# A planned two-branch kernel: other pairs in seven-product form, another order of the input splits, two rows normed on GpSimd, longer planned transposes

## The chip, the core and the metric

The kernel runs on one core of one Trainium2 chip. Its time is the device time of one execution in microseconds (us). The profile adds one recorded execution, in which every instruction of every engine has a start and an end. The engines are TensorE (PE in the profile), VectorE (DVE), ScalarE (ACT), GpSimd (POOL) and SyncE (SP), which only issues DMAs.

## The reference

```python
xn = _layernorm(x, axis=-1)                       # x = A_q, 2048 rows of 1024
return x + _A_ref(xn, ...) + _B_ref(xn, B_w1, B_w2)

# _A_ref: k_shift is a 4-tap causal convolution of k by channel
kv = k_shift * v
y = irfft(rfft(pad(kv)) * rfft(pad(ssm_k)))[:S]   # a long causal convolution by channel
y = y + kv * ssm_D
return xn * y

# _B_ref
h = silu(xn @ w1)                                 # w1 is 1024 x 3584
return h @ w2                                     # w2 is 3584 x 1024
```

All inputs and outputs are float32. There are 2048 rows, 1024 channels and 3584 hidden columns.

## The kernel before

**Two branches, one TensorE.** The feed-forward branch (B) is two large products; the convolution branch (A) runs as transforms, whose first stages are products with constant matrices. All products are made from float16 halves: a value is scaled and split into a high part (ScalarE, L355) and a low part (VectorE, L347, the function `split`), and each product takes three matmuls, high by high, high by low and low by high. L930 to L932 are these three of the first feed-forward product, L1062 to L1064 of the second, L1529 to L1531 of the convolution's forward transform (constants `cfw`), L1721 to L1723 of its inverse (`civ`).

**Seven products for eight.** The normed input is cut into 2 by 2 blocks, A11 to A22, by halves of its rows and of its columns, and so is each 256-column pair of w1, B11 to B22. Sums of blocks (S1 to S4 of the input, T1 to T4 of the weights) let a unit make its block products from seven products P1 to P7 (`PRODUCTS`) in place of eight. The hidden columns are 14 such pairs. In the first half of the rows, pairs 0 and 1 are done as plain products ahead of all others, because their operands are there first: first with A11 and A12 (rows 0 to 3), then with A21 and A22 (rows 4 to 7). Units 2 to 13 follow, and then units 0 to 13 for the second half of the rows (rows 8 to 15).

**Pairs.** The second product, h by w2, is itself made in seven-product form for four of the 14 pairs, those in `PAIRS`. For them the activations need further sums and splits on VectorE and ScalarE, written by `quad`; the others take `blocks`. The hidden columns of the other ten pairs (`PLAIN`) go through the plain second product, and those of `PAIRS` come last of all.

**The start.** `ln_rows` takes statistics of rows (`bn_stats`, L497 and L499), a square root on ScalarE, and applies the norm with one VectorE `tensor_scalar` a row (L516). `transposes` turns the rows with TensorE into PSUM (L535; a ring of three buffers). `first_rows` splits A11 and A12; `lower_sums` makes A21, A22 and S1, `upper_sums` makes S2, S3 and S4, and `give` hands each to a `split`. `scales_w1` finds the scale of a weight pair with `norm` (a matmul at L451 and a chain of small VectorE operations), and `factors_w1` makes and splits its factors. The eight places `x0` to `x7` in SBUF are shared: places 0 and 1 first hold the raw weights of pairs 0 and 1, and later S1 and S4 (`XPLACE`).

**The convolution.** For each of eight groups of 128 channels, `signal_parts` splits the signal into the one buffer `cm`; a transposing DMA (`X`, L337) moves it into `hl`, where the matmuls of the forward transform read it; `cm` can be refilled only when that DMA has read it. Sums on VectorE over `spec` and `tmp`, a product of the spectra and an inverse follow, and `gated` writes the result with an accumulating DMA issued by GpSimd (`G`, L341; tile `yt`, or a free `wo`). The results of the second product reach the output by such DMAs too.

**A planner sets every queue.** The kernel is written as many streams (Python generators) that yield operations, `Op(engine, busy, late, emit, reads, writes, margin)`. `Order.run` takes again and again the operation that could start first by its own model of time, less a `bias` of its stream, and emits it. So the order of the instructions on each engine follows from the costs and biases that the streams declare. Where the model sees TensorE idle, it puts filler matmuls in (L327):

```python
if op.fill is not None and t > 45.0:
    for _ in range(int(((t - self.free[op.eng]) * 0.7 - 0.3) / 0.22)):
        op.fill()
```

For a DMA the model takes the later of `busy + late` and a common pipe of all DMAs:

```python
self.pipe = max(self.pipe, t + 3.0) + op.nbytes / 330e3
done = end = max(end, self.pipe + 0.2)
```

The hardware runs each engine's queue in that order, and an instruction waits for what it needs.

Of the kernel before, what the change touches and what calls it, by code (L numbers as in the profile page):

```python
# [13 lines left out]
F16 = mybir.dt.float16  # L14
I32 = mybir.dt.int32
AF = mybir.ActivationFunctionType
# [23 lines left out]
            "P5": ("S1", "T1"), "P3": ("S4", "B22"), "P4": ("A22", "T4")}  # L40
XPLACE = dict(A11=2, A12=3, A22=5, S1=0, S2=6, S3=7, S4=1)

PAIRS = (8, 9, 12, 13)
NQ = len(PAIRS)
PLAIN = [j for j in range(NF) if j // 2 not in PAIRS]
NC = len(PLAIN) // 4
# [59 lines left out]
class Order:  # L106
# [27 lines left out]
    def add(self, gen, bias, floor=0.0):  # L134
        s = Stream(gen, bias, floor)
        self.streams.append(s)
        self.advance(s)
# [154 lines left out]
def h3_ffn_kernel(ctx, tc, x, kp, vs, fs, shift, dskip, w1, w2, cfwd, cinv, out):  # L292
# [23 lines left out]
    def V(f, o, ins, us=None, m=0.15):  # L316
        return Op("DVE", us or 1.03 * (size(o) / 960 + 0.075), 0.16, f, ins, [o], m)
# [16 lines left out]
    def X(o, i, m=0.3):  # L334

        n = size(o) * o.shape[0] * mybir.dt.size(o.dtype)
        return Op("SP", 0.6, 0.1, lambda: nc.sync.dma_start(o, i, transpose=True), [i], [o], m, n)  # L337

    def G(o, i, m=0.3):
        n = size(i) * i.shape[0] * mybir.dt.size(i.dtype)  # L340
# [135 lines left out]
    def load_row(t):  # L476
# [5 lines left out]
            yield L(xts[t][0][:, q], xr[t // T2, t % T2][:, q])  # L482
        flag["xt", t].set()

    def ln_rows():
        for t0, n, bias in ((0, 2, 0.26), (2, 2, 0.17), (4, 4, 0.15), (8, 8, 0.03)):
            yield bias
            q = slice(t0, t0 + n)
            mv = lnp.tile([P, 2, 8], F32, name="mv", bufs=2)
            m = mv[:, :, 0:n]  # L490
            order_in = (8, 9, 12, 13, 10, 11, 14, 15) if n == 8 else range(t0, t0 + n)
            for t in order_in:
                yield flag["xt", t]
                xt = xts[t][0]
                st = lnp.tile([P, 2, 6], F32, name="st", bufs=2)
                for a in range(2):
                    yield V(lambda: nc.vector.bn_stats(st[:, a, :], xt[:, a * W:(a + 1) * W]), st[:, a, :],  # L497
                            [xt[:, a * W:(a + 1) * W]], us=0.65)
                yield V(lambda: nc.vector.bn_aggr(stat[:, t, :], st), stat[:, t, :], [st], us=0.2)  # L499

            def chain(m=m, q=q):
                v = stat[:, q, 1]
                nc.vector.reciprocal(m[:, 0, :], m[:, 0, :])
                nc.vector.tensor_mul(m[:, 1, :], m[:, 0, :], m[:, 0, :])
                nc.vector.scalar_tensor_tensor(m[:, 1, :], v, 1e-5, m[:, 1, :], op0=ADD, op1=MUL)
                nc.vector.tensor_scalar(m[:, 1, :], m[:, 1, :], -0.5, 1.5, op0=MUL, op1=ADD)
                nc.vector.tensor_mul(rstd[:, q], m[:, 0, :], m[:, 1, :])
                if n == 8:
                    nc.vector.scalar_tensor_tensor(nmr, stat[:, :, 0], -1.0, rstd, op0=MUL, op1=MUL)
            yield a_act(m[:, 0, :], stat[:, q, 1], AF.Sqrt, bias=eps)  # L510
            p = V(chain, rstd[:, q], [stat[:, q, :], m[:, 0, :]], us=0.8)
            p.writes += [m[:, 0, :], m[:, 1, :]] + ([nmr] if n == 8 else [])
            yield p
            for t in order_in:
                xt = xts[t][0]
                yield V(lambda: nc.vector.tensor_scalar(xt, xt, stat[:, t, 0:1], rstd[:, t:t + 1], op0=SUB, op1=MUL),  # L516
                        xt, [xt, stat[:, t, :], rstd[:, t:t + 1]], us=0.78)
                flag["xn", t].set()

    pts = []  # L520
# [56 lines left out]
    def give(to, name, src, tok):  # L577

        put = to(name)
        if put is None:  # L580
            tok.set()
        else:
            add(put(src, tok), to.bias)

    def lower_sums(to, ring):

# [36 lines left out]
    def x_rows():  # L623
        yield from first_rows()
        second["A21"], second["tok"] = places[4].tile([P, 4, KH, 2, P], F16)
        for name in ("A22", "S2", "S3", "S1", "S4"):
            r = places[XPLACE[name]]
            yield r.ready
            xo[0][name], xtok[0][name] = r.tile([P, 4, KH, 2, P], F16)

        class Kept:
            bias = 0.14

            def __init__(self, i):
                self.i = i

            def __call__(self, name):
                if name in ("A11", "A12"):
                    return None
                o = (second["A21"] if name == "A21" else xo[0][name])[:, self.i]  # L640
                return lambda src, tok: split(o[:, :, 0], o[:, :, 1], src, XS, (tok, flag["x", 0, name]))

        yield 0.14
        half = []
        for i in range(4):
            half.append((yield from lower_sums(Kept(i), s1_r)))
        Kept.bias = 0.11
        yield 0.11
        for i in range(4):
            yield from upper_sums(Kept(i), xst_r, *half[i], t=i)  # L650

        class Spilled(Kept):
            bias = 0.02

            def __call__(self, name):
                return None if name == "A21" else lambda src, tok: spill(xsp[name][:, self.i], src, tok)

        def spill(o, src, tok):
            yield lambda: s1_r.ready() or xst_r.ready()
            r = s1_r if s1_r.ready() else xst_r  # L660
            st, stok = r.tile([P, KH, 2, P], F16)
            yield from split(st[:, :, 0], st[:, :, 1], src, XS, (tok,))
            yield L(o, st)
            stok.set()
            flag["spilled"].set()

        yield 0.02
        for i in range(4):
            part = yield from lower_sums(Spilled(i), sums_r)
            yield from upper_sums(Spilled(i), sums_r, *part)  # L670
        flag["x done"].set()
# [34 lines left out]
    def scales_w1():  # L706
        for n, (_, i) in enumerate(pairs):
            yield (0.25, 0.16, 0.1, 0.05)[min(n, 3)]
            m = 4 if n == 0 else 2
            if n >= NP:  # L710
                for a in range(m):
                    yield flag["raw", n, a]
                flag["scaled", n].set()
                continue
            yield sq_r.ready
            ss, tok = sq_r.tile([P, 4])
            for a in range(m):
                yield flag["raw", n, a]
                r = raws[n][2][a]
                yield a_act(junk[:, 0:r.shape[1]], r, AF.Square, total=ss[:, a:a + 1])  # L720

            def then(e, i=i):
                sc = wsc[:, i]
                nc.vector.tensor_scalar(sc[:, 3:5], powers[:, 3:5], e, None, op0=MUL)
                nc.vector.reciprocal(e, e)
                nc.vector.tensor_scalar(sc[:, 0:3], powers[:, 0:3], e, None, op0=MUL)
            yield from norm(ctxs["nm"], ss[:, 0:m], (m,), then, ([wsc[:, i]], [flag["scaled", n], tok]))

    spills = []

# [1067 lines left out]

    warm = lnp.tile([P, 1], F32, name="warm")
    nc.scalar.activation(warm, ones[:, 0:1], AF.Sqrt)  # L1800
    add(begin(), 0.05)
    add(warm_up(), 0.0)
    add(x_rows(), 0.03)
# [53 lines left out]
```

## Time and profile before

| | |
|---|---|
| runs | 1257.01, 1260.42, 1257.72 us |
| median of the three | 1257.72 us |
| the profiled execution's own time | 1257.19 us |
| its span, first to last instruction | 1255.4 us |
| mean granted TensorE clock | 0.996 |
| TensorE busy | 1233.6 us (98%) |
| VectorE busy | 1147.3 us (91%) |
| ScalarE busy | 731.0 us (58%) |
| GpSimd busy | 132.6 us (11%) |

A busy time is the union of an engine's instructions. A row of the time line gives start, duration, engine, line, operation, what it writes and reads, and in square brackets how long the engine stood idle before it and what released it. A row of waits gives who waited for whom, the total in us, how often, and the longest. One kernel matmul of float32 operands shows as two records.

### The profile page before, as it was taken

The page shows a single profiled execution, that of the slowest core. Times are in us where ns is not written, and L with a number is a line of the kernel's source. Part 1 is how long each engine was busy: PE and PEld are TensorE (multiplying, and loading weights), DVE is VectorE, ACT ScalarE, POOL GpSimd, SP SyncE. Part 2 cuts the span into 40 slices and gives each one's busy share as a digit, 9 for nine tenths or more (in the row PEclk, how much of TensorE's full clock was granted, in tenths as well). Part 3 has the DMA queues.
Part 4 walks back from the last instruction along what each step waited for, and adds up shares of the span by engine and source line. Part 5 has one row for each costly group of instructions (what it writes and reads, how often), then busy time and mean ns, then how long its engine had stood idle before and what let it go on. Part 6 is the DMA issues. An engine that isn't in the chain of part 4 may idle for free.

```text
span 1255.4 us, 17118 instructions
## 1 busy us (share of the span) xinstructions
PE 1233.6 (98%) x6058; PEld 599.7 (48%) x6058; DVE 1147.3 (91%) x1517; ACT 731.0 (58%) x1165; POOL 132.6 (11%) x141
## 2 busy tenths in 40 slices
PE   7999999999999999999999999999999999899998
PEld 6544554444444544445444544544454454345444
DVE  7999997999899979999999899989989979898994
ACT  6868887878767776748752632463173264426222
POOL 0000000000000020002010300210030030113114
PEclk9999999999999999999999999999999999999999
DMA  9358889889999998879998887699597578978777
GB/s 334 94 185 293 288 297 315 285 278 325 337 335 281 264 286 262 267 224 239 352 316 209 168 270 180 147 265 263 116 220 172 129 171 245 227 157 140 163 143 92
DMA packets 254293, 292.93 MB, mean 233 GB/s; under 512 B 48768, under 2 KB 167808, under 8 KB 252032
## 3 DMA queue, kind: packets, MB, share of 16 engines
q1 hardware_dynamic: 227472, 266.93, 67.9%
q0 software_dynamic: 26736, 24.92, 15.5%
q8 instruction: 47, 0.77, 0.2%
q14 instruction: 38, 0.31, 0.1%
HBM read 193.22 MB, written 98.57 MB: 232 GB/s over the span
## 4 chain that ended last, share of the span: by engine, by line
PE 72%; DVE 9%; DMA 5%; issue 2%; ACT 1%; POOL 0%; SPq 0%; DVEq 0%; ACTq 0%; POOLq 0%
PE ff L1062 11%; PE ff L1063 11%; PE ff L1064 11%; PE ff L930 11%; PE ff L931 11%; PE ff L932 11%; DVE spec L344 3%; DMA hl<-cm 2%; PE ps L1529 2%; PE ps L1531 2%; PE ps L1530 2%; DVE x L347 1%; DMA out<-yt 1%; DVE acc L347 1%; PE ps L1723 1%
## 5 line engine op out<-in xcount | busy, mean ns | idle before, releaser
L1062 PE MATMUL ff<-x,wo 128*128 128x512 f16 x868 | 328.8, 379 | 3.8 <-ACT hf L355 3.2
L1063 PE MATMUL ff<-x,wo 128*128 128x512 f16 x868 | 328.8, 379 | 0.0
L1064 PE MATMUL ff<-x,wo 128*128 128x512 f16 x868 | 328.6, 379 | 0.0
L931 PE MATMUL ff<-x,wo 128*128 128x512 f16 (+1 forms) x808 | 303.4, 375 | 2.7 <-DVE x L347 2.7
L932 PE MATMUL ff<-x,wo 128*128 128x512 f16 (+1 forms) x808 | 303.5, 376 | 1.9 <-DVE wo L347 1.9
L930 PE MATMUL ff<-x,wo 128*128 128x512 f16 (+1 forms) x808 | 303.5, 376 | 1.5 <-ACT wo L355 1.5
L344 DVE TENSOR_TENSOR spec<-spec 128x1024 f32<-128x1024 f32 (+2 forms) x272 | 263.6, 1000 | 2.7
L1063 PEld LDWEIGHTS <-wo 128*128 128x128 f16 x868 | 85.0, 98 | 103.8 <-issue 4.8
L1064 PEld LDWEIGHTS <-wo 128*128 128x128 f16 x868 | 85.0, 98 | 102.1 <-issue 0.8
L1062 PEld LDWEIGHTS <-wo 128*128 128x128 f16 x868 | 85.9, 99 | 99.8 <-issue 0.8
L932 PEld LDWEIGHTS <-wo 128*128 128x128 f16 x808 | 79.2, 98 | 98.0 <-issue 3.4
L930 PEld LDWEIGHTS <-wo 128*128 128x128 f16 x808 | 80.7, 100 | 88.8 <-ACT wo L355 1.7
L931 PEld LDWEIGHTS <-wo 128*128 128x128 f16 x808 | 79.3, 98 | 87.6
L355 ACT ACTIVATE hf<-ff,invc 128x512 f32<-128x512 f32 x60 | 40.9, 683 | 114.2 <-PE ff L1064 89.4
L341 POOL DMA_DIRECT2D out<-hf x59 | 51.8, 879 | 468.5 <-ACT hf L355 429.5
L341 POOL DMA_DIRECT2D out<-yt x56 | 62.2, 1274 | 321.0 <-DVE yt L347 186.3
L344 DVE TENSOR_TENSOR tmp<-spec 128x2048 f32<-128x2048 f32 (+1 forms) x48 | 92.5, 1933 | 1.0
L355 ACT ACTIVATE spec<-spec 128x1024 bf16<-128x1024 f32 x32 | 33.7, 1054 | 73.2 <-DVE spec L344 73.1
L347 DVE SCALAR_TENSOR_TENSOR ht<-hf,wsc,ht 128x1024 f16<-128x1024 f32 (+1 forms) x56 | 67.3, 1202 | 8.4 <-ACT ht L355 8.2
L347 DVE SCALAR_TENSOR_TENSOR acc<-kin,taps,acc 128x1024 f32<-128x1024 f32 x48 | 61.4, 1279 | 4.4 <-ACT acc L355 4.3
L355 ACT ACTIVATE spec<-ps 128x512 f32<-128x512 f32 x96 | 55.6, 590 | 15.2 <-PE ps L1531 11.4
L355 ACT ACTIVATE ht<-hf,wsc 128x1024 f16<-128x1024 f32 (+1 forms) x56 | 60.8, 1086 | 5.9 <-DVE hf L344 2.2
(173 smaller groups left out, 1756.6 us busy)
## 6 DMA issues: line engine op xcount, KB each, us to landing
wo<-hs SPq DMA_DIRECT2D x160, 256.0 KB, 3.6
hs<-ht SPq DMA_DIRECT2D x80, 256.0 KB, 4.7
wraw<-in_w SPq DMA_DIRECT2D x31, 512.0 KB, 5.5
out<-hf POOLq DMA_DIRECT2D x59, 256.0 KB, 4.4
raw<-in_w SPq DMA_DIRECT2D x28, 512.0 KB, 5.6
kin<-in_kp SPq DMA_DIRECT2D x16, 704.0 KB, 5.9
kf<-in_fs SPq DMA_DIRECT2D x8, 1024.0 KB, 6.0
hsfS<-ht SPq DMA_DIRECT2D x32, 256.0 KB, 4.2
```

The source lines that it names most:

```text
L341: return Op("POOL", 1.1, 4.8, lambda: nc.gpsimd.dma_start(o, i, accum_op=ADD), [i], [o], m, n)
L344: return V(lambda: nc.vector.tensor_tensor(o, a, b, op=op), o, [a, b], **k)
L347: return V(lambda: nc.vector.scalar_tensor_tensor(o, a, s, b, op0=op0, op1=op1), o, [a, b] + ([] if isinstance(s, float) else [s]), **k)
L355: nc.scalar.activation(o, i, func, scale=scale, **kw)
L930: nc.tensor.matmul(o, w[:, 0, k], xf[:, :, k, 0], start=first and k == 0, stop=False, **kw)
L931: nc.tensor.matmul(o, w[:, 0, k], xf[:, :, k, 1], start=False, stop=False, **kw)
L932: nc.tensor.matmul(o, w[:, 1, k], xf[:, :, k, 0], start=False, stop=last and k == KH - 1, **kw)
L1062: nc.tensor.matmul(o, hx[:, n, 0, :], wc[:, n, 0, q], start=first and n == 0, stop=False, **kw)
L1063: nc.tensor.matmul(o, hx[:, n, 0, :], wc[:, n, 1, q], start=False, stop=False, **kw)
L1064: nc.tensor.matmul(o, hx[:, n, 1, :], wc[:, n, 0, q], start=False, stop=last and n == 3, **kw)
L1529: nc.tensor.matmul(o, cf[:, 0], hi[i], start=i == 0, stop=False, **kw)
L1530: nc.tensor.matmul(o, cf[:, 0], lo[i], start=False, stop=False, **kw)
```

## The change

It does six things.

- `PAIRS` is (4, 5, 12, 13) in place of (8, 9, 12, 13).
- The transposing DMA `X` is declared to be late by 6.0 us in place of 0.1, so that the planner counts at least 6.6 us from its issue to its end. The DMA itself is the same.
- The norms of rows 6 and 7 are applied on GpSimd.
- In `give`, the splits of A21 and A22 get a bias higher by 0.03 and those of S1 to S4 a lower one, while the stream's bias is over 0.1 (the first half of the rows).
- `x_rows` waits for the place of S4 only ahead of `upper_sums`.
- The matmul that sums the squares of the first weight pair is declared ready 1.2 us sooner, and the planner starts with the square-root table as loaded, as it is.

```diff
--- before.py
+++ after.py
@@ -40,7 +40,7 @@
             "P5": ("S1", "T1"), "P3": ("S4", "B22"), "P4": ("A22", "T4")}
 XPLACE = dict(A11=2, A12=3, A22=5, S1=0, S2=6, S3=7, S4=1)
 
-PAIRS = (8, 9, 12, 13)
+PAIRS = (4, 5, 12, 13)
 NQ = len(PAIRS)
 PLAIN = [j for j in range(NF) if j // 2 not in PAIRS]
 NC = len(PLAIN) // 4
@@ -334,7 +334,7 @@
     def X(o, i, m=0.3):
 
         n = size(o) * o.shape[0] * mybir.dt.size(o.dtype)
-        return Op("SP", 0.6, 0.1, lambda: nc.sync.dma_start(o, i, transpose=True), [i], [o], m, n)
+        return Op("SP", 0.6, 6.0, lambda: nc.sync.dma_start(o, i, transpose=True), [i], [o], m, n)
 
     def G(o, i, m=0.3):
         n = size(i) * i.shape[0] * mybir.dt.size(i.dtype)
@@ -482,6 +482,8 @@
             yield L(xts[t][0][:, q], xr[t // T2, t % T2][:, q])
         flag["xt", t].set()
 
+    LNPOOL = (6, 7)
+
     def ln_rows():
         for t0, n, bias in ((0, 2, 0.26), (2, 2, 0.17), (4, 4, 0.15), (8, 8, 0.03)):
             yield bias
@@ -513,8 +515,13 @@
             yield p
             for t in order_in:
                 xt = xts[t][0]
-                yield V(lambda: nc.vector.tensor_scalar(xt, xt, stat[:, t, 0:1], rstd[:, t:t + 1], op0=SUB, op1=MUL),
-                        xt, [xt, stat[:, t, :], rstd[:, t:t + 1]], us=0.78)
+                def apply(e):
+                    return lambda: e.tensor_scalar(xt, xt, stat[:, t, 0:1], rstd[:, t:t + 1], op0=SUB, op1=MUL)
+                ins = [xt, stat[:, t, :], rstd[:, t:t + 1]]
+                if t in LNPOOL:
+                    yield Op("POOL", 1.3, 0.3, apply(nc.gpsimd), ins, [xt], 0.3)
+                else:
+                    yield V(apply(nc.vector), xt, ins, us=0.78)
                 flag["xn", t].set()
 
     pts = []
@@ -580,7 +587,7 @@
         if put is None:
             tok.set()
         else:
-            add(put(src, tok), to.bias)
+            add(put(src, tok), to.bias + (0.03 if name in ('A21', 'A22') else -0.03) * (to.bias > 0.1))
 
     def lower_sums(to, ring):
 
@@ -623,10 +630,14 @@
     def x_rows():
         yield from first_rows()
         second["A21"], second["tok"] = places[4].tile([P, 4, KH, 2, P], F16)
-        for name in ("A22", "S2", "S3", "S1", "S4"):
-            r = places[XPLACE[name]]
-            yield r.ready
-            xo[0][name], xtok[0][name] = r.tile([P, 4, KH, 2, P], F16)
+
+        def have(*names):
+            for name in names:
+                r = places[XPLACE[name]]
+                yield r.ready
+                xo[0][name], xtok[0][name] = r.tile([P, 4, KH, 2, P], F16)
+
+        yield from have("A22", "S2", "S3", "S1")
 
         class Kept:
             bias = 0.14
@@ -644,6 +655,7 @@
         half = []
         for i in range(4):
             half.append((yield from lower_sums(Kept(i), s1_r)))
+        yield from have("S4")
         Kept.bias = 0.11
         yield 0.11
         for i in range(4):
@@ -724,7 +736,7 @@
                 nc.vector.tensor_scalar(sc[:, 3:5], powers[:, 3:5], e, None, op0=MUL)
                 nc.vector.reciprocal(e, e)
                 nc.vector.tensor_scalar(sc[:, 0:3], powers[:, 0:3], e, None, op0=MUL)
-            yield from norm(ctxs["nm"], ss[:, 0:m], (m,), then, ([wsc[:, i]], [flag["scaled", n], tok]))
+            yield from norm(ctxs["nm"], ss[:, 0:m], (m,), then, ([wsc[:, i]], [flag["scaled", n], tok]), 0.3 if n == 0 else 1.5)
 
     spills = []
 
@@ -1798,6 +1810,7 @@
 
     warm = lnp.tile([P, 1], F32, name="warm")
     nc.scalar.activation(warm, ones[:, 0:1], AF.Sqrt)
+    order.table = AF.Sqrt
     add(begin(), 0.05)
     add(warm_up(), 0.0)
     add(x_rows(), 0.03)
```

In the changed program the instructions on TensorE, VectorE, ScalarE, GpSimd and SP are the same in kind and number, but for 6 filler matmuls fewer (4 in place of 10) and two `tensor_scalar` on GpSimd that were on VectorE. The planner gives all of them a new order from the start on. Twelve lines of code are added, so a line of the convolution has a number higher by 12.

## The prediction

> **What bounds the kernel now.** I read the page's head first, then busy time by stretch, then TensorE's waits, and only then the time lines of the places that these name.
>
> ```profile
> span 1255.4 us, 17118 instructions
> PE 1233.6 (98%) x6058; PEld 599.7 (48%) x6058; DVE 1147.3 (91%) x1517; ACT 731.0 (58%) x1165; POOL 132.6 (11%) x141
> 0.00:62.00 62.00, 51.12 (x324) 36.63 (x325) 54.22 (x123) 47.29 (x83) 0.70 (x6) 0.97 0.64 216
> 62.00:256.00 194.00, 193.81 (x943) 93.37 (x941) 181.25 (x301) 152.52 (x222) 0.95 (x1) 1.00 0.82 277
> 256.00:1255.40 999.40, 988.68 (x4795) 469.73 (x4793) 911.81 (x1095) 531.18 (x861) 130.94 (x134) 1.00 0.85 226
> PE ff L1062 <- ACT hf L355: 3.2, 1, 3.2
> PE ff L931 <- DVE x L347: 2.7, 3, 1.1
> PE ff L932 <- DVE wo L347: 1.9, 2, 1.1
> PE ps L1529 <- ACT tmp L355: 1.7, 1, 1.7
> ```
>
> The stretch rows give length, then PE, PEld, DVE, ACT and POOL busy, clock, DMA share and GB/s. TensorE is the bound: idle 10.9 us of the first 62, 0.2 of the next 194, 10.7 of the last 999. The change leaves TensorE's real products as they are; it removes 6 of 10 filler matmuls, moves two vector instructions to GpSimd, and reorders every queue. So only three things can move: the idle time and fillers at the start, the few later waits, and the tail behind the last matmul. The change has at most some 20 us to win, and no such limit to what it can lose.
>
> **The start.** Between 36 and 55 us VectorE is never idle and TensorE runs out of work. The rows show VectorE's queue from the norms of rows 4 to 7 to the last split of A21, and TensorE waiting for it.
>
> ```profile
> 36.16 2.98 DVE L516 TENSOR_SCALAR xt<-xt,stat,rstd 128x1024 f32<-128x1024 f32 x4
> 45.30 0.68 DVE L344 TENSOR_TENSOR t<-raw 128x512 f32<-128x512 f32 x1
> 45.90 0.68 DVE L347 SCALAR_TENSOR_TENSOR x<-ft,x 128x512 f16<-128x512 f32 x1
> 48.89 0.68 DVE L347 SCALAR_TENSOR_TENSOR x<-s,x 128x512 f16<-128x512 f32 x1
> 49.49 0.68 DVE L347 SCALAR_TENSOR_TENSOR x<-ft,x 128x512 f16<-128x512 f32 x1
> 50.69 0.68 DVE L344 TENSOR_TENSOR raw<-raw,raw 128x512 f32<-128x512 f32 x1
> 51.40 0.69 DVE L344 TENSOR_TENSOR raw<-raw 128x512 f32<-128x512 f32 x1
> 52.01 0.68 DVE L344 TENSOR_TENSOR s<-ft,s 128x512 f32<-128x512 f32 x1
> 53.81 1.28 DVE L347 SCALAR_TENSOR_TENSOR x<-ft,x 128x512 f16<-128x512 f32 x2
> 50.72 2.40 PE L327 MATMUL ff<-one,zero 128*128 128x128 f32 x20
> 53.08 0.38 PE L930 MATMUL ff<-x,wo 128*128 128x512 f16 x1
> 54.55 0.38 PE L931 MATMUL ff<-x,wo 128*128 128x512 f16 x1 [1.09 <-DVE x L347]
> ```
>
> The matmul at 54.55 needs the low half of the last A21 split, first of the pair at 53.81. In the new order the same stretch of the queue lacks: two norms, 2.98 / 4 x 2 = 1.49 us (to GpSimd); one S1 split, 0.60 from start to start (48.89 to 49.49), which A21 and A22 now pass; and three differences of weights that now follow that split, 0.60 (45.30 to 45.90), 0.71 (50.69 to 51.40) and 0.61 (51.40 to 52.01). Together 4.0 us. The other instructions between the two points are the same in kind and number. The late place for S4 and the forward bias of A21 and A22 are what lets these splits pass; they cost nothing themselves.
>
> Ahead of that stretch the weights' scales move forward of a batch-norm half and the first product may start some 2 us sooner, but the second half of that product hangs on rows 2 and 3, whose norms stand at the same place of VectorE's queue: adding its rows up to 36 us I get the norms of rows 4 to 7 some 0.2 us later than before (0.5 either way). So the last A21 split comes 4.0 - 0.2 = 3.8 us sooner. TensorE itself reaches the fillers at 50.72 now; with 4 fillers (8 of the 20 records, 0.96 us) and no other gain it would be ready at 51.7, a gain of 2.9. The gain is thus 2.9 to 3.8; I take 3.4. What hides VectorE's work now postponed (three differences, one split, 2.5 us) is the run of four A21 and A22 products per weight pair, 96 matmuls; the first seven-product unit wants S3 after them, and by the rows it is there about 1.4 us ahead. Without that cover, 2.5 us come back.
>
> GpSimd's norm is not in the trace. The nearest row of GpSimd handles 128 columns:
>
> ```profile
> 1.02 0.29 POOL masks.py:199 TENSOR_SCALAR_AFFINE_SELECT ident<-ident 128x128 f32<-128x128 f32 x1
> ```
>
> Eight times that is 2.3 us a row of 1024; VectorE's own 0.75 is the low end. I take 2.3: row 6 would be there at about 38.7, row 7 at 41.0. Adding rows along the new queue, TensorE's transposes of row 6 wait for a transpose buffer until about 42, those of row 7 until 46, so both are hidden up to some 5 us a row. By the Trainium skill, GPSIMD Engine Reference, section 3.1, at 1.8 to 2.6 cycles an element and 1.2 GHz, an estimate for the row would be 1.5 to 2.2 us; the sum would stay as it is.
>
> **The one long wait.** The last third holds the biggest single loss: a transposing DMA of cm lands late, ScalarE waits to refill cm's only buffer, and the PSUM copies queued behind that wait hold up TensorE.
>
> ```profile
> 1079.93 2.06 SPq L337 DMA_TRANSPOSE hl<-cm  x1
> 1090.62 0.72 ACT L355 ACTIVATE cm<-acc,csc 128x512 f16<-128x512 f32 x1 [4.37 <-DMA hl<-cm]
> 1092.58 0.58 PE L1062 MATMUL ff<-x,wo 128*128 128x512 f16 x1 [3.17 <-ACT hf L355]
> 1095.52 0.60 PE L1063 MATMUL ff<-x,wo 128*128 128x512 f16 x1
> 1095.94 0.39 PE L1064 MATMUL ff<-x,wo 128*128 128x512 f16 x1
> 1096.17 0.38 PE L1062 MATMUL ff<-x,wo 128*128 128x512 f16 x1
> ACT cm L355 <- DMA hl<-cm: 32.0, 12, 5.3
> DMA to landing us min/median/max: 3.0/4.6/10.7
> ```
>
> The wait is 3.2 us, and after it eight matmuls start 0.42 apart (1095.52 to 1095.94) where 0.22 follows (1095.94 to 1096.17): 8 x 0.21 = 1.7 more, 4.9 in all. The order now allows 6.6 us from a transpose's issue instead of about 4, where 4.6 is the median landing. In the new queues the third transpose of this group is no longer followed by loads of w2, which are through by then, and three PSUM copies stand between the third cm and the fourth. I take the whole 4.9 as gone; the ends are 4.9 and 0, if a landing of 10.7 hits a tight place again.
>
> **The pairs.** In each half of the rows a seven-product group of pairs 4 and 5 has on VectorE, beyond what a plain one has, one split of 1024, one of 512 and four sums: 1.2 + 0.66 + 4 x 0.60 = 4.3 us. In the first half 8.5 us so move from the units at 170 to 206 us to those at 98 to 135.
>
> ```profile
> 100.00:120.00 20.00, 20.00 (x103) 10.26 (x102) 19.32 (x36) 15.86 (x22) 0.00 (x0) 1.00 0.83 274
> 180.00:200.00 20.00, 20.00 (x96) 9.24 (x94) 16.83 (x26) 16.40 (x24) 0.00 (x0) 1.00 0.75 262
> ```
>
> VectorE is full (19.3 of 20) where they go and has room (16.8) where they leave. What gives way are the statistics, norms and sums of rows 8 to 15, which the planner serves last and no product needs before the second half; weight factors come first. I take 0; without that cover TensorE would wait by up to 8.5.
>
> **The convolution starts later.** In the second half the same 8.5 us move ahead of the convolution's first groups, and the pushed-back rows hold its start. In TensorE's queue the first forward transform of group 0 stands behind 1409 matmuls instead of 1352, of groups 1 and 2 51 and 28 later, of group 3 3 earlier. At 0.2155 a matmul, VectorE must do the same three groups in some 12.9 us less.
>
> ```profile
> 278.00:424.00 146.00, 146.00 (x681) 66.50 (x680) 137.08 (x168) 104.41 (x161) 0.76 (x1) 1.00 0.99 314
> 424.00:672.00 248.00, 247.32 (x1199) 117.20 (x1198) 228.98 (x271) 168.40 (x265) 23.75 (x23) 1.00 0.94 276
> ```
>
> VectorE idled 8.9 + 19.0 = 27.9 us there; 15 would be left. That is enough on the sum, but part of the idleness is waiting for DMAs that do not shrink. The bounds are 0 and 12.9; I take 1.7, one wait of the kind that the trace has already (TensorE for tmp).
>
> **The tail.** The last inverse transform is followed by 45 matmuls instead of 72, so its GpSimd writes end the queue.
>
> ```profile
> 1238.59 2.21 POOL L341 DMA_DIRECT2D out<-wo  x2 [0.18 <-issue]
> 1248.68 0.88 POOL L341 DMA_DIRECT2D out<-wo  x1 [1.34 <-ACT wo L355]
> 1250.11 1.73 SPq L332 DMA_DIRECT2D out<-hf  x2
> out<-wo POOLq DMA_DIRECT2D x8, 128.0 KB, 3.4
> out<-yt POOLq DMA_DIRECT2D x56, 128.0 KB, 5.5
> out<-hf SPq DMA_DIRECT2D x2, 128.0 KB, 3.2
> ```
>
> Now the end is SP's second write, begun near 1251.5 and landing 3.2 later, 1254.7. In the new queue three convolution writes follow the copied product that is issued at 1248.68: with 0.88 + 0.2 for that and 1.2 each for two, the third is issued at 1252.2 and lands at 1255.6 with 3.4, at 1257.7 with 5.5. So 0.9 (0 if they run ahead, 3.0 at most).
>
> **The sum.** -3.4 - 4.9 + 1.7 + 0.9 = -5.7 us against the profiled execution's 1257.19 (its span and 1.8 around it): 1251.5. That run lies 0.5 below the median of 1257.72, so the forecast is 1252.0.
>
> **Rivals.** *The forecast's case*, 0.55: each term near its value, from 1249.0 (-3.8 - 4.9 alone) to about 1253.9.
>
> *The convolution is late* (slower), 0.17: VectorE's idle time in groups 0 to 2 does not shrink, and TensorE waits for the forward transforms by the whole 12.9: -3.4 - 4.9 + 0.9 + 12.9 = +5.5, 1263.2. It decides from 7.4 us of such waits, where the sum is zero. For it: VectorE is 94% busy there, DMA share 0.94 to 0.99; against it: TensorE waited under 1 us there now.
>
> *The long transposes still bite*, 0.16: the allowance is below the 10.7 that does the harm, and the 4.9 recurs at another group: -0.8, 1256.9.
>
> *GpSimd holds up VectorE*, 0.12: both norms run beside VectorE's queue, and if that stands still for their 4.6 us, the start's gain of 3.4 turns into -1.2, the sum is -1.1, 1256.6. For it speaks that VectorE has no idle time there to absorb it; nothing in the trace shows the two together. The Trainium skill, GPSIMD Engine Reference, section 1, says that the two share their SBUF interfaces and contend when VectorE reads two SBUF inputs or runs in a 2-port mode; no run here shows it yet.
>
> About 0.3%, 3.8 us, is what a measurement can tell. The first case is faster, the last two are the same, the second is slower: 0.55, 0.28, 0.17. The range takes the low end 1249.0 with a little for the median's place, and at the top reaches past 1256.9 toward the late convolution: 1248.5 to 1260.5.
>
> **What would show it.** L931 (L943 then) behind the fillers at about 51 us instead of 54.55, with eight filler records; two GpSimd rows of 128x1024 near 36.5, 5 us or less each. TensorE's granted clock 1.00 after 1000 us, no wait of 3 us for hf; ScalarE's waits for cm well under 32.0 in sum. Waits at L1529 (L1541 then) between 290 and 700 us above 7 in sum would mean the late convolution. Three GpSimd writes behind the last copy show the tail. The forecast is wrong if the start's gain is there and is used up by new waits after 256 us, or if VectorE's instructions near 37 to 41 us stretch.

## The result and the profile after

The changed kernel takes 1262.12 us (median of 7 runs, 1260.45 to 1262.92) against 1257.72 us before (7 runs beside it, 1256.28 to 1260.42): the ratio is 1.0038, interval 1.0022 to 1.0054. It is 4.4 us slower. The forecast was 1252.0, and 1262.12 lies above its range too. The profiled execution took 1262.68 us with a span of 1260.9, so the two spans to compare are 1260.9 and 1255.4.

The head of the page of the changed kernel, the longest of TensorE's waits in it (one of 1.9 us at the start is left out), and ScalarE's wait for cm:

```profile
span 1260.9 us, 17109 instructions
PE 1232.5 (98%) x6046; PEld 598.5 (47%) x6046; DVE 1144.7 (91%) x1515; ACT 731.2 (58%) x1165; POOL 141.2 (11%) x143
PE ft L542 <- issue: 2.7, 1, 2.7
PE ps L1541 <- DVE tmp L344: 2.3, 2, 1.3
PE ft L542 <- ACT xt L355: 2.2, 1, 2.2
PE ff L943 <- DVE x L347: 2.0, 2, 1.2
PE ff L1074 <- DVE hf L347: 1.7, 2, 1.1
ACT cm L355 <- DMA hl<-cm: 11.6, 6, 5.6
```

The one wait of 3.2 us for hf is gone, as forecast, and ScalarE's waits for cm fall from 32.0 to 11.6 us. In their place stand many waits of about 1 us, most of them for VectorE. The stretches of the changed kernel (length, then PE, PEld, DVE, ACT and POOL busy, clock, DMA share, GB/s):

```profile
0.00:62.00 62.00, 50.94 (x315) 35.95 (x316) 52.06 (x118) 46.32 (x83) 9.12 (x8) 0.94 0.64 216
62.00:256.00 194.00, 193.93 (x944) 93.49 (x943) 182.09 (x304) 154.53 (x222) 0.99 (x1) 1.00 0.84 278
290.00:700.00 410.00, 407.09 (x1941) 189.78 (x1940) 379.26 (x455) 269.72 (x423) 26.21 (x26) 1.00 0.95 280
1096.00:1180.00 84.00, 81.02 (x400) 39.06 (x399) 75.56 (x89) 33.76 (x57) 22.64 (x24) 1.00 0.79 151
```

TensorE idles 2.9 us from 290 to 700 and 3.0 us from 1096 to 1180. The same stretches of the kernel before, for the two that are new:

```profile
290.00:700.00 410.00, 408.16 (x1947) 190.49 (x1945) 381.68 (x458) 271.14 (x426) 26.27 (x26) 1.00 0.93 280
1096.00:1180.00 84.00, 84.00 (x416) 40.63 (x415) 77.50 (x89) 33.07 (x55) 21.79 (x23) 1.00 0.80 151
```

Idle time alone misses fillers, and matmuls at half clock (the granted clock is 0.54 from 30 to 32 us in the changed kernel, 0.51 from 1093 to 1096 us in the kernel before), so I also count TensorE's useful work. Every matmul has its steady distance to the next (0.216 us for 512 columns, 0.109 for 256 columns or a 128-column pass in float32); fillers and warm-up count nothing. The lag at a time is what the kernel before has done by then less what this kernel has done. Negative is ahead.

| lag, us, at | 62 | 290 | 705 | 1085 | 1096 | 1180 | last matmul ends | behind it |
|---|---|---|---|---|---|---|---|---|
| before | | | | | | | 1250.95 | 4.47 |
| changed | -0.65 | -0.65 | 1.74 | 2.38 | -1.73 | 1.73 | 1252.71 | 8.17 |

So the 5.46 us between the spans are: start -0.65, convolution up to 1085 us +3.0, the wait near 1092 -4.1, the 84 us behind it +3.5, and the stretch behind the last matmul +3.7. The convolution's two parts make +6.5.

**The start.** First the square root for rows 2 and 3 in the kernel before:

```profile
19.50 0.28 ACT L355 ACTIVATE mv<-stat,eps 128x2 f32<-128x2 f32 x1
```

Rows of the changed kernel from 22 to 54 us, in order of time over the engines:

```profile
22.26 0.28 ACT L355 ACTIVATE mv<-stat,eps 128x2 f32<-128x2 f32 x1
23.57 1.54 DVE L519 TENSOR_SCALAR xt<-xt,stat,rstd 128x1024 f32<-128x1024 f32 x2
28.14 0.91 PE L542 MATMUL ft<-ident,xt 128*128 128x128 f32 x4 [2.18 <-ACT xt L355]
28.85 0.42 PE L942 MATMUL ff<-x,wo 128*128 128x256 f16 x1
29.06 0.42 PE L943 MATMUL ff<-x,wo 128*128 128x256 f16 x1
35.86 0.16 DVE L457 TENSOR_REDUCE pow<-nm 128x1 f32<-128x2 f32 x1 [0.86 <-PE nm L451]
38.04 2.33 DVE L519 TENSOR_SCALAR xt<-xt,stat,rstd 128x1024 f32<-128x1024 f32 x2
38.12 8.42 POOL L519 TENSOR_SCALAR xt<-xt,stat,rstd 128x1024 f32<-128x1024 f32 x2 [36.81 <-DVE rstd L509]
51.61 1.06 PE L327 MATMUL ff<-one,zero 128*128 128x128 f32 x8
53.02 1.44 DVE L347 SCALAR_TENSOR_TENSOR x<-ft,x 128x512 f16<-128x512 f32 x2
53.76 0.38 PE L943 MATMUL ff<-x,wo 128*128 128x512 f16 x1 [0.80 <-DVE x L347]
```

The four fillers are there (8 records), but L943 starts at 53.76 and not at 51, only 0.8 us sooner than before. ScalarE's root for rows 2 and 3 comes at 22.26; TensorE later stands idle 2.2 us and starts 256-column matmuls 0.21 apart (28.85 to 29.06) instead of 0.11; the kernel before has such a stretch too, from 18.0 to 20.8 us. The norms of the next rows begin at 38.04 instead of 36.16. GpSimd takes 4.2 us a row, and VectorE's two rows beside it take 1.17 us each instead of 0.75.

**The last groups.** The scale of a group's result starts with L457 on VectorE. The row of the last group in the time line of the changed kernel:

```profile
1223.61 0.15 DVE L457 TENSOR_REDUCE pow<-ps 128x1 f32<-128x4 f32 x1
```

The same row in the kernel before:

```profile
1215.87 0.15 DVE L457 TENSOR_REDUCE pow<-ps 128x1 f32<-128x4 f32 x1
```

VectorE's chain is 7.7 us later than before in the last group, and 5.4 us in the seventh (1132.23 against 1126.79), while TensorE, at 1120 us, is 0.4 us ahead. Over the eight groups the same chain is late by 13.2, 6.4, 1.3, 2.4, 5.3, 6.3, 5.4 and 7.7 us. So VectorE has almost caught up in the third group and falls behind again from the fifth on.

**The tail.** GpSimd's last writes in the changed kernel, and SyncE's:

```profile
1247.80 0.88 POOL L341 DMA_DIRECT2D out<-hf  x1 [2.71 <-DVE wo L347]
1248.40 4.33 POOL L341 DMA_DIRECT2D out<-wo  x4
1254.61 2.22 POOL L341 DMA_DIRECT2D out<-wo  x2 [1.88 <-issue]
1251.87 1.73 SPq L332 DMA_DIRECT2D out<-hf  x2
```

SyncE's second write no longer sets the end. GpSimd still has seven writes to issue from 1247.8 on, stops 1.9 us between the fifth and the sixth with no releaser in the profile, and its queue ends at 1256.83.

The trace's landings show what the stop waits for. The sixth write begins 0.31 us after the second has landed (1254.3), the seventh 0.31 us after the third (1255.0), and it is so in six more executions with 45 matmuls behind the last inverse transform. A write of the convolution goes out in 256 pieces of 512 bytes, one of the feed-forward product in 128 pieces of 2048. In all 13 traces GpSimd's DMAs never have more than 896 pieces begun and not landed, and a write that would make them 1024 begins only after a landing. No run varied this, so the limit is a reading that every write fits and not a tested cause.

### The profile page after: what moved, and what is told of

It reads as the page before. It is cut to its first block, busy times and chain, and to the rows that moved or that the text cites. A ratio compares the mean times of both kernels' runs of the same rounds, so it can differ in the third digit from the quotient of the medians.

```text
span 1260.9 us, 17109 instructions
## 1 busy us (share of the span) xinstructions
PE 1232.5 (98%) x6046; PEld 598.5 (47%) x6046; DVE 1144.7 (91%) x1515; ACT 731.2 (58%) x1165; POOL 141.2 (11%) x143
## 4 chain that ended last, share of the span: by engine, by line
PE 67%; DVE 21%; DMA 6%; issue 4%; ACT 2%; POOL 0%; SPq 0%; POOLq 0%; DVEq 0%; ACTq 0%
PE ff L942 12%; PE ff L943 12%; PE ff L944 12%; DVE spec L344 7%; PE ff L1074 7%; PE ff L1075 7%; PE ff L1076 7%; DVE tmp L344 3%; DVE x L347 3%; PE ps L1541 1%; PE ps L1542 1%; PE ps L1543 1%; DVE acc L347 1%; DMA out<-yt 1%; DMA hf<-in_w 1%
## 5 line engine op out<-in xcount | busy, mean ns | idle before, releaser
L943 PE MATMUL ff<-x,wo 128*128 128x512 f16 (+1 forms) x808 | 303.5, 376 | 2.0 <-DVE x L347 2.0
L943 PEld LDWEIGHTS <-wo 128*128 128x128 f16 x808 | 79.3, 98 | 88.5 <-issue 1.2
```

Source lines behind the costliest of these rows:

```text
L943: nc.tensor.matmul(o, w[:, 0, k], xf[:, :, k, 1], start=False, stop=False, **kw)
```

## The experiments

### Which edit costs what: four kernels

```diff
 # e1_pairs: before, with
-PAIRS = (8, 9, 12, 13)
+PAIRS = (4, 5, 12, 13)
 # e2_late: before, with
-        return Op("SP", 0.6, 0.1, ...transpose=True...)
+        return Op("SP", 0.6, 6.0, ...transpose=True...)
 # e3_start: the changed kernel, with both of these as before
 # e4_noroot: the changed kernel, with
-            yield from norm(..., 0.3 if n == 0 else 1.5)
+            yield from norm(...)
-    order.table = AF.Sqrt
```

> The kernel before with one edit: the seven-product groups are pairs 4, 5, 12 and 13. The comparison of the two traces gives four terms of the 5.5 us between the spans: first 62 us -0.65, convolution +6.5, the wait at 1092 -4.1, behind the last matmul +3.7. Theory A: the convolution's part and the tail come with the pairs. Then the first 62 us stay as before within 0.3, at 290 to 700 us TensorE loses 2.5 us or more against before, and the tail behind the last matmul is 8.2 us instead of 4.5, since the new queue again holds 45 instead of 72 matmuls behind the last inverse transform. Time 1261 to 1264.5 if the wait at 1092 stays, 1257 to 1260.5 if it goes. Rival B: the convolution's waits come from the start (GpSimd's rows, the order of A21 and A22) or from the long transposes; then the stretch from 290 to 700 us loses under 1 us here.

> The kernel before with one edit: the planner takes 6.0 instead of 0.1 us for a transposing DMA's landing. Start as before within 0.3. Theory A: the wait at 1092 goes (-4.1 to -4.9), and the tail is 8.2 us (45 matmuls behind the last inverse), +3.7. Open is the stretch from 1096 to 1180 us, where the changed kernel loses 3.5 us to waits for VectorE. If these are the other side of the wait that was taken away (VectorE had caught up in it), they are here too: time 1260 to 1262. Rival: they come with the pairs; then 1256 to 1258.

> The changed kernel with the old pairs and the old landing time, so all edits of the start alone. Theory A: first 62 us 0.4 to 1.0 shorter than before, since ScalarE takes the square root of rows 2 and 3 behind two passes of squares (22.3 instead of 19.5 us); tail 8.2 us, +3.7 (45 matmuls behind the last inverse); convolution from 290 to 700 within 1 us of before; the wait at 1092 stays. Time 1260 to 1262. Rival B: the start edits make the convolution late; then 290 to 700 us loses 2.5 or more and the time is 1263 to 1266.

> The changed kernel without two edits, the norm's margin of 0.3 and the activation table given at the start; these reorder only the first 200 matmuls. Theory A: they are what cost the start: ScalarE takes the root of rows 2 and 3 at 19.5 again, rows 2 and 3 are normed some 2.2 us sooner, TensorE does not fall to half clock at 28 us, and the first 62 us are 2.2 to 3.4 us shorter than in the changed kernel; all else as there. Time 1258.5 to 1260. Rival C: VectorE's work, not TensorE's start, sets when the convolution ends, and the start's gain is lost in later waits: then 1261.5 to 1262.5, as the changed kernel.

| kernel | median, us | ratio to before | lag at 62 | 290 | 705 | 1085 | 1096 | 1180 | behind the last matmul |
|---|---|---|---|---|---|---|---|---|---|
| e1_pairs | 1263.62 | 1.0055 (1.0036 to 1.0073) | 0.43 | 0.86 | 2.29 | 3.89 | -0.22 | 1.94 | 8.51 |
| e2_late | 1260.93 | 1.0030 (1.0016 to 1.0043) | 0.22 | 0.22 | 1.85 | 1.94 | -2.59 | 1.08 | 8.46 |
| e3_start | 1263.87 | 1.0048 (1.0036 to 1.0061) | -1.73 | -1.08 | 4.88 | 6.91 | 2.81 | 5.18 | 8.58 |
| e4_noroot | 1260.64 | 1.0025 (1.0016 to 1.0035) | -2.16 | -2.16 | 1.64 | 2.16 | -2.59 | 0.86 | 8.64 |

The long transposes alone (e2_late) go as their theory A said, with the waits for VectorE behind 1096 us. For the pairs and for the start's edits neither theory stands in full. Each of the three parts makes the kernel slower by itself, and each brings much the same pattern: 1.4 to 6.0 us lost between 290 and 705, the wait near 1092 gone, waits for VectorE behind it, and a tail of 8.5 us. The pairs alone lose 1.4 us there, less than the 2.5 expected; the start alone loses 6.0, in size rival B, but at one place: its planner put nine fillers near 529 us (18 records), TensorE waits 2.8 us for VectorE ahead of them, and the next product starts only at 532.68.

```profile
529.14 3.69 PE L327 MATMUL ff<-one,zero 128*128 128x128 f32 x18 [2.81 <-DVE hf L344]
```

The three edits touch different instructions. What their kernels share is the planner's order: in all of them it puts 45 instead of 72 matmuls behind the last inverse transform, and moves the forward transforms. What e1_pairs writes differs from the reference's output by 0.069 of it, and no run shows why, so only its times are of use here.

VectorE's chain tells two delays apart. In e2_late the scales of the first two groups are only 0.8 and 1.0 us late, and yet those of the last four are 6.0, 5.8, 4.9 and 7.2 us late, about as in the changed kernel. The late half of the delay therefore comes with the later order and is not a debt from the first groups.

In e4_noroot the root comes at 19.8 us again and the first 62 us are 1.5 us shorter than in the changed kernel, as theory A said, though less than the 2.2 expected; three more executions of the changed kernel's start (in the experiments below) are 0.4 to 1.3 us behind it. From 290 to 705 it loses 3.8 us where the changed kernel loses 2.4, with a wait of 2.4 us for a transposing DMA of cm at 334 us, so at 705 the two stand 0.1 apart. Its median is still 1.5 us lower.

### The tail alone

```diff
             for b in range(2):
-                yield G(out4[b][...], yt[:, b])
+                w = G(out4[b][...], yt[:, b])
+                if g == NG - 1 and t in TO[-2:]:
+                    w.emit = lambda b=b: nc.sync.dma_start(out4[b][...], yt[:, b])
+                yield w
```

> The changed kernel in its own order, but the last four writes of the convolution's last group go out from SyncE's queue as plain writes instead of from GpSimd's as adding ones, so those blocks of the output lack the feed-forward's part. Theory: the 8.2 us behind the last matmul are GpSimd's queue, which still has six writes of about 1.1 us to issue behind the last copies and stops once for 1.9 us. Then the tail falls to 4.5 to 5.5 us (before: 4.5) and the time by 2.7 to 3.7 us against the changed kernel, to 1258.5 to 1259.5. Rival: the tail is set by the late copies and the landing of the last block; then it stays above 7 us and the time within 1 us.

Measured 1258.38 us, ratio to before 1.0003 (0.9992 to 1.0014): 3.7 us under the changed kernel, with every other instruction in its place. The end of GpSimd's queue:

```profile
1245.61 0.88 POOL L341 DMA_DIRECT2D out<-hf  x1 [2.82 <-DVE wo L347]
1246.21 1.17 POOL L341 DMA_DIRECT2D out<-wo  x1
1248.18 0.89 POOL L341 DMA_DIRECT2D out<-wo  x1 [0.80 <-ACT wo L355]
```

GpSimd has three writes where it had seven, and the 1.9-us stop is gone. The stretch behind the last matmul is 5.9 us in the profiled execution, a little over the 5.5 expected: SyncE's queue now has four writes more among its last. So the tail is GpSimd's queue. Its size is less sure: the medians differ by 3.7 us, as much as the tail had grown, but in the two traces the tail shrinks by 2.3 us, and the other 2.3 us between them come earlier, where the two orders are the same. Whether it is the adding writes or the place in GpSimd's queue that costs the time, this experiment does not tell apart.

### Room on VectorE

```diff
             for n in range(4):
-                yield v_tt(run(tmp, 0, 16), ..., MUL)
+                w = v_tt(run(tmp, 0, 16), ..., MUL)
+                if n % 2:
+                    w.emit = lambda: None
+                yield w
```

> The changed kernel in its own order, but every second of the first multiplications of the products (128x2048, 2.29 us on VectorE, 16 of 32) is left out, so half of the products are not those of the reference. This gives VectorE 4.6 us in each of the eight groups. Theory: TensorE's waits in the convolution (584, 1101, 1145 and 1156 us, 4.3 us together, and the shorter ones) are VectorE being too full; they go, and the time falls by 3 to 5 us to 1257 to 1259, with the wait for the transposing DMA at 334 us and the 8.2 us of tail left as they are. Rival: the waits come from transfers or from ScalarE; they stay and the time falls by under 1 us.

Measured 1257.05 us, ratio to before 0.9987 (0.9975 to 0.9999), 5.1 us under the changed kernel. TensorE's waits from 1090 to 1200 us (who waited for whom, total, times, longest) in the changed kernel:

```profile
PE ff L1074 <- DVE hf L347: 1.1, 1, 1.1
PE ps L1541 <- DVE tmp L344: 1.0, 1, 1.0
PE ps L1734 <- DVE zl L347: 0.9, 1, 0.9
```

The same list with the room:

```profile
PE ff L1074 <- DVE hf L347: 1.7, 1, 1.7
PE ps L1541 <- DVE tmp L344: 0.3, 1, 0.3
```

The waits near 1145 and 1156 go, the one near 1100 stays (1.7 us at 1097.8), and so does the 1.34 us at 584. The lag no longer grows: -1.5 at 290, -1.7 at 705, -1.1 at 1085, -3.7 at 1180. The tail stays at 8.22 us. So the time that the convolution loses is in large part VectorE's, but not every wait of it. The same room was not given to the kernel before, so how much of the 5.1 us the change itself had cost is not shown.

### The wait put back

```diff
                 nc.tensor.matmul(o, hx[:, n, 0, :], wc[:, n, 0, q], ...)
+                done[0] += 1
+                if done[0] == 657:
+                    for _ in range(19):
+                        nc.tensor.matmul(o[:, 0:P], zeros, ones, start=False, stop=False, **kw)
```

> The changed kernel in its own order, but TensorE gets 19 filler matmuls (0.22 us each, 4.2 us, adding zero) at about 1092 us, where the kernel before waits for the transposing DMA (4.1 to 4.9 us). Theory: the wait that the change took away and the waits for VectorE at 1101, 1145 and 1156 us (3.5 us) are two sides of one thing, since VectorE's queue is what sets this stretch; then these waits shrink to under 1 us, and the time rises by 0 to 1.2 us. Rival: they are separate; then the time rises by 3.5 to 4.2 us, to about 1266.

Measured 1261.74 us, ratio to before 1.0033 (1.0018 to 1.0049). With 4.2 us of fillers on the bounding engine the time is not above the changed kernel's 1262.12. TensorE's waits from 1050 to 1200 us in it (lines shifted by five):

```profile
PE ff L1075 <- ACT ff L356: 1.1, 1, 1.1
PE ps L1546 <- DVE tmp L345: 0.4, 1, 0.4
```

The waits at 1101, 1145 and 1156 shrink from 3.0 us to 0.4. The theory holds and the rival's 1266 is out: the long wait of the kernel before was time in which VectorE caught up, and taking it away gives most of the time back within 90 us. It does not give back all of it. In the trace, where the fillers begin at 1095.2, the lag grows by 1.1 us from 1085 to 1180, and in the changed kernel it falls by 0.65; so about 2.4 of the 4.2 us are hidden there, and the medians can't tell a cost of 0 from one of 1.7. (The profiled execution took 1266.6 us, 4.9 above the median; 4.1 us of it are lost between 290 and 340 us.)

### The last inverse put ahead

```diff
 # e4_noroot, with
+                if g == NG - 1:
+                    yield 1.0
                 yield from inverse(g)
-            if op.fill is not None and t > 45.0:
+            if op.fill is not None and 45.0 < t < 100.0:
```

> The changed kernel without the norm's margin and the given table, and with the inverse of the last group put ahead (a bias of 1.0, with the planner's fillers kept to the first 100 us), which leaves 63 instead of 45 matmuls behind the last inverse transform and the order of GpSimd's last writes as before. Theory: the tail returns to 4.5 to 5.5 us, TensorE loses at most 1.5 us more in waits for the last group; time 1257 to 1259, no slower than before. Rival: VectorE can't deliver the last group sooner, TensorE waits 3 us or more at 1200 to 1245 us instead, and the time stays at 1260 to 1261.

Measured 1265.34 us, ratio to before 1.0048 (1.0030 to 1.0066), 4.7 us above e4_noroot. The tail does shrink, to 5.05 us, and TensorE pays for it:

```profile
1221.13 5.08 DVE L344 TENSOR_TENSOR spec<-spec 128x1024 f32<-128x1024 f32 x7
1226.24 2.36 DVE L347 SCALAR_TENSOR_TENSOR spec<-spec 128x1024 f32<-128x1024 f32 x2
1228.52 2.35 DVE L344 TENSOR_TENSOR spec<-spec 128x1024 f32<-128x1024 f32 x2
1230.79 0.74 DVE L347 SCALAR_TENSOR_TENSOR hf<-ff,invc,hf 128x512 f32<-128x512 f32 x1
1231.59 0.58 PE L1074 MATMUL ff<-x,wo 128*128 128x512 f16 x1 [5.49 <-DVE hf L347]
```

The inverse's sums now stand ahead of the copy of hf that TensorE needs, and it waits 5.5 us. The rival holds in kind, and the time is worse than it said. The short tail of the kernel before goes with VectorE being ready with the last group's scale some 8 us sooner; putting the inverse ahead in the new order doesn't buy it.

### The start with the rest left in its old order

With the late place for S4 and GpSimd's rows alone, the planner's order is that of the kernel before for TensorE's instructions from 183 us on (86% of its matmuls), with 72 of them behind the last inverse; six fillers fewer stand in the part ahead. That lets the start be measured by itself.

```diff
 # e10_two: before, with
+    LNPOOL = (6, 7)
...
-        for name in ("A22", "S2", "S3", "S1", "S4"):
+        yield from have("A22", "S2", "S3", "S1")
...
+        yield from have("S4")
 # e11_rows: e10_two, same plan, with
-                    yield Op("POOL", 1.3, 0.3, apply(nc.gpsimd), ins, [xt], 0.3)
+                    yield Op("POOL", 1.3, 0.3, apply(nc.vector), ins, [xt], 0.3)
 # e12_four: e10_two, with the norm's margin of 0.3 and order.table = AF.Sqrt
```

> The kernel before with two edits of the change alone: rows 6 and 7 normed on GpSimd, and S4's place taken late. In this queue nothing moves after the first third but for 6 fewer fillers: the forward and inverse transforms stand in before's order, with 72 matmuls behind the last inverse. Theory: the start's term was right (2.2 to 3.0 us in the first 62 us) and what cost the changed kernel its time is the later order of the convolution and of the tail, so this one keeps the gain: 1254.5 to 1256, faster than before, with the tail at 4.5 us. Rival: VectorE, not TensorE, sets the convolution's time, and the start's gain comes back as waits from 290 us on; then 1257 to 1258.

> As the one with the two edits, in the same order, but rows 6 and 7 are normed on VectorE at the place in its queue where the planner put them for GpSimd. Theory: GpSimd's rows (4.2 us each in the changed kernel) save VectorE 1.5 us but slow its own two rows beside them from 0.75 to 1.17 us, so the net is 0.6 to 0.7 us: the last split of A21 comes 0.4 to 0.9 us later than with GpSimd, and the time is 0 to 0.9 us more. Rival: sharing costs VectorE more than the two rows; then it is faster on VectorE.

> As the one with the two edits, and also the norm's margin of 0.3 and the given activation table, which reorder the first 200 matmuls only. Theory: these two edits cost the start 1.2 to 1.5 us by themselves (the root of rows 2 and 3 behind two passes of squares on ScalarE, TensorE idle and then at half clock at 26 to 32 us): first 62 us 1.0 to 1.6 us longer, time 1 to 1.5 us more than with the two edits. Rival: what was seen between kernels of other orders was chance; then within 0.3 us.

| kernel | median, us | ratio to before | lag at 62 | behind the last matmul |
|---|---|---|---|---|
| e10_two | 1256.23 | 0.9989 (0.9976 to 1.0002) | -0.65 | 4.61 |
| e11_rows | 1256.36 | 0.9989 (0.9976 to 1.0002) | -0.86 | 5.03 |
| e12_four | 1256.71 | 0.9994 (0.9984 to 1.0004) | -0.65 | 4.72 |

With the order kept, the tail stays short: these are the lowest medians of all complete kernels, 5.4 to 5.9 us under the changed kernel. Against before their intervals reach 1, so a gain of 1.1 to 1.6 us is not shown. The start is worth less than I expected, 0.65 to 0.86 us at 62 and not 2.2, and in the traces even that does not last. At 290 us the three stand 1.7, 1.1 and 0.7 us behind the kernel before. TensorE's waits from 62 to 300 us in e10_two, where the kernel before has only one of 0.2 us:

```profile
PE ff L942 <- ACT hf L355: 1.5, 1, 1.5
PE ft L542 <- DVE pow L457: 0.7, 1, 0.7
```

The first is at 228 us, where the queue is before's again, the second at 165 us; e11_rows and e12_four have both (1.4 and 0.7 us, 0.7 and 0.7 us). So e10_two's theory, that the start's gain is kept, fails: the gain comes back, and sooner than its rival had it. The three traces also show the long wait near 1092 again. It is 2.5 to 3.2 us long there, and in e10_two fifteen matmuls start 0.43 apart behind it, in the other two none, so its price differs from execution to execution. (The profiled execution of e10_two took 1261.0 us, 4.8 above its median.) GpSimd's rows make no difference in time (0.1 us), as e11_rows' theory allowed. VectorE's norms and the last pair of splits of A21 in e11_rows, from the time line:

```profile
36.45 2.26 DVE L519 TENSOR_SCALAR xt<-xt,stat,rstd 128x1024 f32<-128x1024 f32 x3
39.29 0.81 DVE L519 TENSOR_SCALAR xt<-xt,stat,rstd 128x1024 f32<-128x1024 f32 x1
50.37 1.29 DVE L347 SCALAR_TENSOR_TENSOR x<-ft,x 128x512 f16<-128x512 f32 x2
```

The same in e10_two, with GpSimd's rows:

```profile
37.11 2.34 DVE L519 TENSOR_SCALAR xt<-xt,stat,rstd 128x1024 f32<-128x1024 f32 x2
37.18 8.43 POOL L519 TENSOR_SCALAR xt<-xt,stat,rstd 128x1024 f32<-128x1024 f32 x2 [35.87 <-DVE rstd L509]
42.48 1.08 DVE L347 SCALAR_TENSOR_TENSOR wo<-x,wsc,wo 128x512 f16<-128x512 f32 x1
50.73 1.28 DVE L347 SCALAR_TENSOR_TENSOR x<-ft,x 128x512 f16<-128x512 f32 x2
```

From the first norm to the last pair of splits VectorE needs 13.9 us with four rows and 13.6 with two. Of the 1.5 us that two rows take, 1.2 come back as slower instructions: two rows at 1.17 instead of 0.75, and one split of weights at 1.08 instead of 0.75. In e12_four the margin and the table cost nothing in the first 62 us, against its theory, so the loss that e4_noroot showed belongs to them together with the other order of A21, A22 and S1, not to them alone; 0.5 us between the medians can't be told from none.

## Why the prediction was wrong

**The start, -3.4 forecast, -0.65 measured** (-0.9, -1.3 and -1.7 in the three experiments with the same first 290 us). Two steps failed. "I get the norms of rows 4 to 7 some 0.2 us later": they are 1.9 us later (38.04 against 36.16; 0.9 to 1.7 in the three other executions). I took rows 2 and 3 to stand at the same place of VectorE's queue and didn't look at ScalarE's, where their root went behind two passes of squares, 22.26 instead of 19.50. The second step is "two norms, 1.49 us (to GpSimd)". The norms got 0.65 us shorter by it, 2.98 to 2.33, since the two rows left were slowed. With smaller losses the whole stretch, from the first of these norms to the last pair of A21's splits, shrank from 17.65 to 14.98 us, by 2.7 and not by 4.0; less the 1.9 us of the late norms that leaves the 0.8 us by which L943 is sooner. The 4.2 us a row of GpSimd lie within the 5 that I said would be hidden, but at nearly twice the 2.3 that I took. The estimate from the Trainium skill's GPSIMD Engine Reference, section 3.1, 1.5 to 2.2 us, was lower still, and the measurement decides. The Trainium skill's GPSIMD Engine Reference says in section 1 that GpSimd and VectorE share their SBUF interfaces and contend when VectorE reads two SBUF inputs or runs in a 2-port mode. The trace agrees that the two contend, at 1.17 against 0.75; which of these conditions it was, no run here shows. So the rival of GpSimd holding up VectorE was right in kind: it cost 0.8 us in these rows, not a stop of 4.6.

**The long wait, -4.9 forecast.** It went as forecast (-4.1 at that place) in every one of the new orders. The step that failed is the one that I left out: what is late next. VectorE was; 3.5 us came back by 1180, and e9_hold shows that the wait can be put back at no cost that the medians tell.

**The pairs, 0 forecast.** Right for the first half of the rows: the lag stays -0.65 from 62 to 290.

**The convolution, +1.7 forecast, +6.5 measured.** The mechanism was named and the size was off. I asked whether TensorE would wait at the forward transforms of groups 0 to 2 and set 7 us of such waits as the mark of the late convolution; TensorE idles only 2.9 us from 290 to 700, and loses 2.4 there. The larger part comes where the prediction had no term at all: VectorE, only 1.3 us late in the third group, falls 5 to 8 us behind from the fifth on, and TensorE pays in the last two groups. So the step that failed is to count VectorE's room in groups 0 to 2 alone; e7_relief, with room in every group, gains 5.1 us. The rival came within 1.1 us of the result (1263.2 against 1262.1) by the wrong road.

**The tail, +0.9 forecast, at most 3.0; +3.7 measured.** Three writes behind the last copied product were named, and they are there. I had the third begin at 1252.2, 1.25 us behind the last matmul; it is the second of the pair at 1254.61 and begins near 1255.35, 2.6 us behind it. That is 1.4 more, from the stop of 1.9 us, of which before's trace showed only 0.1 to 0.3 us at a time: I priced the issues that GpSimd had left and not what it had in flight. The other 1.4 us is the landing: I took 3.4 us out of 3.4 to 5.5, and the span ends 5.5 us behind that issue, where the landing and the 0.7 us that follow it in before had made 4.1.

The sum missed 10.1 us against the median. The terms of the profiled spans show where: start 2.75, wait 0.8, convolution 4.8, tail 2.8, together 11.15 of the 11.2 between 1251.5 and the profiled execution's 1262.68.

What stays open: which place in the planner's order makes VectorE late. The pairs alone, the long transposes alone and the start alone each did it; with the two start edits that keep the old order the last group is late by 3.7 us in one trace and early by 0.6 and 0.8 us in the other two. The transposing DMA of cm that lands late at 334 us holds up VectorE in the changed kernel (its next sum of the spectrum waits 5.6 us behind it), but e1_pairs, e2_late and e3_start lose their time without a wait of that size there.

## What to carry to other kernels

- Where a planner sets every queue, the price of an edit is in the order that it sets off far away. Look first at the order of the last stage: how much work stands behind the last result of the slower chain, and how many writes one queue must still issue then.
- With a second engine 91% busy, a wait of the first is also the second's time to catch up. Before counting its removal as a gain, ask whether that engine has room behind it; fillers put in the wait's place are a cheap test.
- Keep the order and change only the engine or the instruction at a place: that measured the tail, GpSimd's rows and the wait one at a time, where whole edits moved everything at once.

## What was not expected of the hardware

- A `tensor_scalar` of 128x1024 in float32 takes 4.2 us on GpSimd and 0.75 on VectorE, and VectorE's same instruction beside it takes 1.17. Of the splits and sums beside GpSimd's rows in e10_two only one split of weights was slower, 1.08 instead of 0.75.
- GpSimd's stop of 1.9 us in the changed kernel (1.7 to 2.6 in six more executions) ends 0.31 us after the landing of an earlier write of its own queue, which no row of the profile names. The kernel before begins eight writes of 256 pieces in a row, about 1.2 us apart, with stops of 0.3 us at most; there each lands 3.3 to 4.0 us after its begin, in the changed kernel's last seven 4.1 to 6.9 us.
- Executions of the same order differ: at 705 us three profiled executions of the changed kernel's order (two of them altered only behind that) have lags of 0.1, 1.7 and 3.8 us. A single trace places a cost; only the medians size it.
